# One decode block on one core: smaller K/V tiles, attention finished in two halves, MLP weights in per-partition blocks, a result in four rows

## The chip, the cores and the metric

The kernel runs on 1 core of one Trainium2 chip. The metric is the device time of one execution in microseconds (us). A profile's span is shorter than the time of the same execution (kernel before: 211.4 and 213.17 us). All runs are single-core runs and are called fast here unless a run says otherwise; one execution of one experiment (a_gate_flat) was slow and is left out of its time and its ratio, and a_strides has one execution, whose state is unknown.

## The reference

One token goes through an attention block with a K/V cache and a gated MLP, both behind a layernorm:

```python
# x [1,1,640]; k_cache, v_cache [1,32,4096,128]; wq [640,4096]; wo [4096,640]
# w_gate, w_up [640,1728]; w_down [1728,640]; all bf16
q = layernorm(x) @ wq                          # 32 heads of 128
p = softmax(q . k_cache / sqrt(128))           # per head, 4096 positions
h = x + (p . v_cache) @ wo
h2 = h + (gelu(layernorm(h) @ w_gate) * (layernorm(h) @ w_up)) @ w_down
```

The two caches are 67 MB of the 84 MB that have to come from memory.

## The kernel before

Eight groups of four heads. For each group one 4 MB tile of K and one of V are loaded into three slots in turn. VectorE multiplies K by q, TensorE folds the products (a matmul with the identity adds up slices), VectorE reduces, ScalarE takes the exponentials, TensorE multiplies by V. Below are parts; `...` marks cuts.

```python
for G in range(NG):                      # NG = 8
    for c in range(2):                   # two 64-row pieces of the K tile
        ...                              # VectorE: prod[c] = K piece * q
        for b in range(16): e.matmul(ps_f[c], id_b, prod[:, c, :, 8*b:8*b+8], ...)   # fold
    load_tile(2 * G + 3, consumed[2 * G])
    for c in range(2): ...               # VectorE reduce_sum, then 4 exponentials on ScalarE
    for c in range(2): ...               # TensorE: 64 matmuls with V
    load_tile(2 * G + 4, consumed[2 * G + 1])

d_wo = dma(arena, A_wo "(p i) n -> p (i n)")                 # after all of K and V
d_wg = dma(wg_sb, B_w_gate "(c p) n -> p c n")               # rows of 3456 bytes
d_wu = dma(wu_sb, B_w_up   "(c p) n -> p c n")
d_wd = [..., dma(wd_sb[:, 0:9], ...), dma(wd_sb[:, 9:13], ...)]   # rows of 1280 bytes
...                                                          # normalise; aP = attention, spread
def proj(e):
    for c in range(5):
        for i in range(32):
            e.matmul(ps_p[:, c:c+1], wo_sb[:, i, c*128:(c+1)*128], aP[:, i:i+1], ...)
...                                                          # h = x + projection; layernorm
e.matmul(ps[0:k, m:m+1], w[:, c, m*128:m*128+k], hlnT[:, c:c+1], ...)     # gate, then up
def resid(e): ...                        # 6 matmuls put h into two rows of 320 columns
def down(ms, last):
    for m in ms:
        for b in range(2):
            e.matmul(ps_d[b][0:1, 0:320], hm[0:k, m:m+1], wd_sb[0:k, m, 320*b:320*b+320], ...)
```

The softmax here doesn't subtract the row's maximum and nothing guards it: scores larger than these inputs give would overflow.

Of the kernel before, what the change touches and what calls it, by code (L numbers as in the profile page):

```python
# [5 lines left out]
FP32 = mybir.dt.float32  # L6
BF16 = mybir.dt.bfloat16
ALU = mybir.AluOpType
ACTF = mybir.ActivationFunctionType
AX = mybir.AxisListType  # L10

D = 640
H = 32
DH = 128
SK = 4096
DF = 1728
# [4 lines left out]
NG = 8  # L21
NSLOT = 3
# [69 lines left out]
def bass_sequential_preLN__gqa_block_cached__glu_gated_geglu__decode_kernel(nc, A_x, A_k_cache, A_v_cache, A_wq, A_wo, B_x, B_w_gate, B_w_up, B_w_down, out):  # L92
    sb = lambda name, shape, dt: nc.alloc_sbuf_tensor(name, shape, dt)
    SLOT = 2 * 5 * DF
    slots = [sb("slot%d" % i, [128, SLOT], BF16) for i in range(NSLOT)]
    arena = sb("arena", [128, 5 * 4096], BF16)
    prod = sb("prod", [128, 2, 64, DH], BF16)
    qb = sb("qb", [128, NG, DH], BF16)
    sc = sb("sc", [128, 2, 64], FP32)
    p_bd = sb("p_bd", [128, 2, 128, 4], BF16)  # L100
    RS = sb("RS", [128, 2, H], FP32)
    x_row = sb("x_row", [1, D], BF16)
    out_row = sb("out_row", [1, D], BF16)
    xx = sb("xx", [128, 10], FP32)
# [4 lines left out]
    hT = sb("hT", [128, 5], FP32)  # L109
    hlnT = sb("hlnT", [128, 5], BF16)  # L110
    rz = sb("rz", [128, H], FP32)
    attnN = sb("attnN", [128, H], BF16)
    aT = sb("aT", [32, 128], BF16)
    aP = sb("aP", [128, 32], BF16)
    sel = sb("sel", [32, 4, 128], BF16)
# [8 lines left out]
    ones_b = sb("ones_b", [128, 512], BF16)  # L124
# [7 lines left out]
    ps_o = bank[2]  # L132
    ps_q = [bank[3], bank[4]]
    ps_d = [bank[3], bank[4]]
# [5 lines left out]
    wo_sb = arena[:, :].rearrange("p (i n) -> p i n", i=32)  # L140
    tile = lambda n: slots[n % NSLOT][:, 0:128 * DH].rearrange("p (g d) -> p g d", d=DH)
# [14 lines left out]
    landed = {}  # L156

    def load_tile(n, *deps):
        src = A_k_cache if n % 2 == 0 else A_v_cache
        g = n // 2  # L160
        src = src[0, 4 * g:4 * g + 4, :, :].rearrange("h (p r) d -> (h p) (r d)", p=32)
        landed[n] = P.dma("sync", slots[n % NSLOT][:, 0:128 * DH], src, *deps)

    for n in range(NSLOT):
        load_tile(n)
# [11 lines left out]
    c_sel = GP(lambda e: e.affine_select(sel[:, :, :], ones_b[0:32, :].rearrange("p (a b) -> p a b", a=4),  # L177
                                         pattern=[[-1, 4], [1, 128]], compare_op=ALU.is_equal,
                                         fill=0.0, base=0, channel_multiplier=-4), c_onesb)
# [4 lines left out]
    def x_cols(e):  # L184
        for c in range(5):
            e.matmul(ps_s[:, c:c + 1], x_row[0:1, c::5], one_bf[0:1, 0:1], start=True, stop=True)
        for c in range(5):
            i = e.matmul(ps_s[:, 5 + c:6 + c], x_row[0:1, c * 128:(c + 1) * 128], one_bf[0:1, 0:1],
                         start=True, stop=True)
        return i  # L190
    xt = T(x_cols, d_x, c_one)
    xc = V(lambda e: e.tensor_copy(xx[:, :], ps_s[:, 0:10]), xt)

    def layernorm(src, ev, out_fn, rd_stats=None):
# [11 lines left out]
    xl = layernorm(xx[:, 0:5], xc, lambda e: e.tensor_scalar(  # L206
        xlnB[:, :, :], xx[:, 0:5].unsqueeze(2).to_broadcast([128, 5, 32]), ln[:, 0:1], ln[:, 4:5],
# [18 lines left out]

    folds, reds, exps, pvs = {}, {}, {}, {}
    consumed = {}
    for G in range(NG):
        kt = tile(2 * G)  # L230
        vt = tile(2 * G + 1)
        for c in range(2):
            t = 2 * G + c
            m = V(lambda e, c=c, G=G, kt=kt: e.tensor_tensor(  # L234
                out=prod[:, c, :, :], in0=kt[:, 64 * c:64 * c + 64, :],
                in1=qb[:, G, :].unsqueeze(1).to_broadcast([128, 64, DH]), op=ALU.mult),
                landed[2 * G], qa, qc, folds.get(t - 2))
            consumed[2 * G] = m

            def fold(e, c=c):  # L240
                for b in range(16):
                    i = e.matmul(ps_f[c][:, :], id_b[:, :], prod[:, c, :, 8 * b:8 * b + 8],  # L242
                                 start=(b == 0), stop=(b == 15))
                return i
            folds[t] = T(fold, m, c_idb, reds.get(t - 2))
        if 2 * G + 3 < 16:
            load_tile(2 * G + 3, consumed[2 * G])
        for c in range(2):
            t = 2 * G + c
            reds[t] = V(lambda e, c=c: e.reduce_sum(  # L250
                sc[:, c, :], ps_f[c][:, :].rearrange("p (g d) -> p g d", d=8), axis=AX.X),
                folds[t], exps.get(t - 2))
            for j in range(4):
                x = A(lambda e, c=c, j=j, G=G: e.activation(  # L254
                    p_bd[32 * j:32 * j + 32, G % 2, 64 * c:64 * c + 64, j], sc[32 * j:32 * j + 32, c, :], ACTF.Exp,
                    bias=zero_t[32 * j:32 * j + 32, 0:1], scale=INV_SQRT_DH,
                    accum_out=RS[32 * j:32 * j + 32, c, 4 * G + j:4 * G + j + 1]),
                    reds[t], pvs.get(t - 4), c_pbd, c_rs, c_eps)
            exps[t] = x
        for c in range(2):  # L260
            t = 2 * G + c

            def pv(e, c=c, G=G, vt=vt):
                for g in range(64 * c, 64 * c + 64):
                    i = e.matmul(ps_o[:, 4 * G:4 * G + 4], vt[:, g, :], p_bd[:, G % 2, g, :],  # L265
                                 start=(g == 0), stop=(g == 127))
                return i
            pvs[t] = T(pv, exps[t], landed[2 * G + 1])
        consumed[2 * G + 1] = pvs[2 * G + 1]
        if 2 * G + 4 < 16:  # L270
            load_tile(2 * G + 4, consumed[2 * G + 1])


    d_wo = P.dma("sync", arena[:, :], A_wo[:, :].rearrange("(p i) n -> p (i n)", i=32), qd)
    sl = slots[16 % NSLOT]
    wg_sb = sl[:, 0:5 * DF].rearrange("p (c n) -> p c n", c=5)
    wu_sb = sl[:, 5 * DF:10 * DF].rearrange("p (c n) -> p c n", c=5)
    d_wg = P.dma("sync", wg_sb, B_w_gate[:, :].rearrange("(c p) n -> p c n", p=128), consumed[13])
    d_wu = P.dma("sync", wu_sb, B_w_up[:, :].rearrange("(c p) n -> p c n", p=128))
    sl2 = slots[17 % NSLOT]  # L280
    wd_sb = sl2[:, 0:14 * D].rearrange("p (c n) -> p c n", c=14)
    wd_v = B_w_down[0:1664, :].rearrange("(c p) n -> p c n", p=128)
    d_wd = [P.dma("sync", wd_sb[0:64, 13, :], B_w_down[1664:1728, :], consumed[14]),
# [3 lines left out]

    def zsum(e):
        e.matmul(ps_z[:, 0:H], ones_f[:, :], RS[:, 0, :], start=True, stop=False)
        return e.matmul(ps_z[:, 0:H], ones_f[:, :], RS[:, 1, :], start=False, stop=True)  # L290
    z = T(zsum, exps[15])
    V(lambda e: e.memset(ps_g[64:128, 13:14], 0.0), reds[15])
    V(lambda e: e.memset(ps_u[64:128, 13:14], 0.0), reds[15])
    z1 = V(lambda e: e.reciprocal(rz[:, :], ps_z[:, 0:H]), z)
    z2 = V(lambda e: e.tensor_mul(attnN[:, :], ps_o[:, 0:H], rz[:, :]), z1, pvs[15])
    ps_t = ps_z[0:32, 64:128].bitcast(BF16)
    z3 = T(lambda e: e.transpose(ps_t, attnN[:, :], id_b[:, :]), z2)
    z4 = V(lambda e: e.tensor_copy(aT[:, :], ps_t), z3)

    def spread(e):  # L300
        for q in range(4):
            i = e.matmul(ps_p[:, 8:40], sel[:, q, :], aT[:, 32 * q:32 * q + 32], start=(q == 0), stop=(q == 3))
        return i
    z5 = T(spread, z4, c_sel)
    z6 = V(lambda e: e.tensor_copy(aP[:, :], ps_p[:, 8:40]), z5)

    def proj(e):
        for c in range(5):
            for i in range(32):
                r = e.matmul(ps_p[:, c:c + 1], wo_sb[:, i, c * 128:(c + 1) * 128], aP[:, i:i + 1],  # L310
                             start=(i == 0), stop=(i == 31))
        return r
    pr = T(proj, z6, d_wo)
    h = V(lambda e: e.tensor_add(hT[:, :], xx[:, 5:10], ps_p[:, 0:5]), pr)  # L314
    hl = layernorm(hT[:, :], h, lambda e: e.tensor_scalar(  # L315
        hlnT[:, :], hT[:, :], ln[:, 0:1], ln[:, 4:5], ALU.subtract, ALU.mult))


    def glu(ps, w):
        def fn(e):  # L320
            for m in range(14):
                k = 128 if m < 13 else 64
                for c in range(5):
                    i = e.matmul(ps[0:k, m:m + 1], w[:, c, m * 128:m * 128 + k], hlnT[:, c:c + 1],  # L324
                                 start=(c == 0), stop=(c == 4))
            return i
        return fn
    ga = T(glu(ps_g, wg_sb), hl, d_wg)
    up = T(glu(ps_u, wu_sb), d_wu)

    def resid(e):
        for (c, lo, hi, b) in ((0, 0, 128, 0), (1, 0, 128, 0), (2, 0, 64, 0), (2, 64, 128, 1), (3, 0, 128, 1), (4, 0, 128, 1)):
            o = c * 128 + lo - 320 * b
            i = e.matmul(ps_d[b][0:1, o:o + hi - lo], hT[:, c:c + 1], id_f[:, lo:hi],  # L334
                         start=(o == 0), stop=False, skip_group_check=True)
        return i
    T(resid, c_idf, h)
# [56 lines left out]
```

## Time and profile before

| | before |
|---|---|
| time, median of 4 runs | 212.28 us (211.7 to 212.78) |
| span of the profiled run | 211.4 us |
| DMA queue 1 | 84.23 MB |
| TensorE / VectorE / ScalarE busy | 59% / 41% / 15% |

The page of the kernel before: the span with its instructions, and the shares that the engines and the DMA have in the chain of waits.

```profile
span 211.4 us, 3675 instructions
...
DMA 58%; PE 24%; DVE 10%; issue 4%; ACT 3%; SPq 1%
```

Windows of the same kernel. The columns are: stretch, its length, busy time of TensorE, its weight loads, VectorE, ScalarE and GpSimd with instruction counts, granted TensorE clock, DMA share, GB/s.

```profile
core 0: us, PE busy (x) PEld busy (x) DVE busy (x) ACT busy (x) POOL busy (x), PEclk, DMA share, GB/s
20.00:40.00 20.00, 10.20 (x95) 5.18 (x96) 10.14 (x4) 2.39 (x11) 0.00 (x0) 1.00 0.98 424
...
202.00:204.00 2.00, 2.00 (x12) 0.84 (x10) 0.00 (x0) 0.00 (x0) 0.00 (x0) 0.50 0.04 10
```

From 20 to 40 us, as in all of the loop, the DMA engines have no idle time (share 0.98); after 202 us next to nothing arrives.

TensorE's timeline (start, length, engine, line, operation, out<-in, shape; in brackets the idle time before it and what ended it): output projection (L310), gate and up (L324), residual (L334), down projection (L353).

```profile
186.06 4.30 PE L310 MATMUL bank<-aP,arena 128*128 128x1 bf16 x156 [1.31 <-DMA arena<-in_A_wo_dram]
192.47 0.27 PE L310 MATMUL bank<-aP,arena 128*128 128x1 bf16 x4 [2.12 <-issue]
...
195.53 3.70 PE L324 MATMUL bank<-hlnT,slot 128*128 128x1 bf16 x121 [1.49 <-DVE hlnT L315]
200.27 0.86 PE L324 MATMUL bank<-hlnT,slot 128*128 128x1 bf16 x19 [1.04 <-issue]
201.06 2.29 PE L334 MATMUL bank<-id_f,hT 128*1 128x128 f32 x12
203.28 5.99 PE L353 MATMUL bank<-slot,hm 64*1 64x320 bf16 x28
```

The down projection is 28 matmuls of one output row in 6.0 us, and it starts when the weights are already there. That is the tail without DMA that the change goes for. The two gaps marked `issue` (2.12 and 1.04 us) are ones in which TensorE waited for nothing that the profile's page shows.

### The profile page before, as it was taken

What the parts mean: (1) busy time and instruction counts of PE and PEld (TensorE: products, weight loads), DVE (VectorE), ACT (ScalarE), POOL (GpSimd) and SP (SyncE); (2) the same over time, 40 slices, a digit from 0 to 9 for tenths busy, and PEclk for the clock granted to TensorE, in tenths of its full rate; (3) what the DMA queues carried; (4) which work ended last, traced back from release to release, by engine and by line L of the source; (5) the groups of instructions that cost most, each with busy time, mean ns of one, the idle gap of its engine ahead of it and who ended that gap; (6) DMA issues with size and microseconds to landing.
All of it is one profiled execution on the core that took longest, in us unless ns stands there. A gap on an engine that the chain in (4) does not pass through costs nothing.

```text
span 211.4 us, 3675 instructions
## 1 busy us (share of the span) xinstructions
PE 125.3 (59%) x1683; PEld 72.8 (34%) x1683; DVE 87.6 (41%) x66; ACT 31.7 (15%) x136; POOL 2.8 (1%) x10
## 2 busy tenths in 40 slices
PE   2304039815970796099449807960994199671896
PEld 1101014611460245035314602450353035571752
DVE  2001295139416911972295159218720962102110
ACT  3001002400330033004202300330042005101000
POOL 5000000000000000000000000000000000000000
PEclk9999999965995599559659955995595569555558
DMA  6999999999999999999999999999999999899800
GB/s 242 443 443 446 409 453 434 403 474 415 394 478 412 409 465 415 414 453 422 425 440 422 431 437 415 446 434 406 447 434 419 440 402 490 348 418 380 301 23 0
DMA packets 5843, 84.46 MB, mean 400 GB/s; under 512 B 386, under 2 KB 2116, under 8 KB 3396
## 3 DMA queue, kind: packets, MB, share of 16 engines
q1 hardware_dynamic: 5826, 84.23, 94.0%
q8 instruction: 13, 0.21, 0.4%
q14 instruction: 2, 0.02, 0.0%
q10 hardware_dynamic: 2, 0.00, 0.0%
HBM read 84.23 MB, written 0.00 MB: 399 GB/s over the span
## 4 chain that ended last, share of the span: by engine, by line
DMA 58%; PE 24%; DVE 10%; issue 4%; ACT 3%; SPq 1%
DMA slot<-in_A_k_cache_dram 42%; DMA arena<-in_A_wo_dram 16%; PE bank L242 13%; DVE prod L234 8%; PE bank L353 3%; PE bank L265 3%; ACT p_bd L254 2%; PE bank L310 2%; PE bank L324 2%; PE bank L334 1%; DVE sc L250 1%; SPq L50 1%; PE bank L198 0%; DVE out_row L359 0%; ACT ln L202 0%
## 5 line engine op out<-in xcount | busy, mean ns | idle before, releaser
L242 PE MATMUL bank<-prod,id_b 128*128 128x512 bf16 x256 | 73.0, 456 | 55.6 <-DVE prod L234 55.6
L234 DVE TENSOR_TENSOR prod<-slot,qb 128x8192 bf16<-128x8192 bf16 x16 | 70.1, 4422 | 44.7 <-DMA slot<-in_A_k_cache_dram 44.7
L242 PEld LDWEIGHTS bank<-prod,id_b 128*128 128x128 bf16 x256 | 28.3, 114 | 97.8 <-DVE prod L234 57.1
L254 ACT ACTIVATE p_bd<-sc,zero_t 32x64 bf16<-32x64 f32 x64 | 27.7, 433 | 133.4 <-DVE sc L250 132.7
L265 PE MATMUL bank<-p_bd,slot 128*128 128x4 bf16 x1024 | 28.5, 165 | 8.1 <-ACT p_bd L254 8.1
L265 PEld LDWEIGHTS bank<-p_bd,slot 128*128 128x128 bf16 x1024 | 27.8, 97 | 10.7 <-ACT p_bd L254 8.8
L250 DVE TENSOR_REDUCE sc<-bank 128x64 f32<-128x512 f32 x16 | 11.1, 692 | 33.6 <-PE bank L242 33.6
L254 ACT ACTIVATION_READ_ACCUMULATOR p_bd<-sc,zero_t 32x1 f32 x64 | 11.8, 184 | 0.0
L218 PE MATMUL bank<-arena,xlnB 128*32 128x512 bf16 x40 | 4.7, 628 | 9.8 <-DMA arena<-in_A_wq_dram 9.8
L310 PE MATMUL bank<-aP,arena 128*128 128x1 bf16 x160 | 4.6, 165 | 3.4 <-issue 2.1
L324 PE MATMUL bank<-hlnT,slot 128*128 128x1 bf16 (+1 forms) x140 | 4.6, 168 | 2.5 <-DVE hlnT L315 1.5
L224 DVE CAST qb<-bank 128x512 bf16<-128x512 f32 x1 | 0.7, 691 | 13.0 <-PE bank L218 13.0
L353 PE MATMUL bank<-slot,hm 128*1 128x320 bf16 (+1 forms) x28 | 6.0, 388 | 0.0
L310 PEld LDWEIGHTS bank<-aP,arena 128*128 128x128 bf16 x160 | 4.4, 104 | 3.6 <-issue 3.6
L218 PEld LDWEIGHTS bank<-arena,xlnB 128*32 128x32 bf16 x40 | 1.3, 133 | 12.4 <-DMA arena<-in_A_wq_dram 6.2
L324 PEld LDWEIGHTS bank<-hlnT,slot 128*128 128x128 bf16 (+1 forms) x140 | 4.4, 107 | 2.7 <-DVE hlnT L315 1.6
L353 PEld LDWEIGHTS bank<-slot,hm 128*1 128x1 bf16 (+1 forms) x28 | 2.7, 102 | 3.4 <-issue 1.0
L359 DVE CAST out_row<-bank 1x320 bf16<-1x320 f32 x1 | 0.5, 479 | 7.4 <-PE bank L353 7.4
L314 DVE TENSOR_TENSOR hT<-xx,bank 128x5 f32<-128x5 f32 x1 | 0.2, 162 | 7.8 <-PE bank L310 7.8
L202 ACT ACTIVATE ln<-ln,eps_t 128x1 f32<-128x1 f32 x2 | 0.6, 294 | 15.9 <-DVE ln L200 15.9
L225 ACT CAST qb<-bank 128x512 bf16<-128x512 f32 x1 | 0.6, 586 | 13.4 <-PE bank L218 13.4
L334 PE MATMUL bank<-id_f,hT 128*1 128x128 f32 (+1 forms) x12 | 2.3, 378 | 0.0
(57 smaller groups left out, 19.0 us busy)
## 6 DMA issues: line engine op xcount, KB each, us to landing
slot<-in_A_k_cache_dram SPq DMA_DIRECT2D x8, 4096.0 KB, 21.8
slot<-in_A_v_cache_dram SPq DMA_DIRECT2D x8, 4096.0 KB, 20.6
arena<-in_A_wo_dram SPq DMA_DIRECT2D x1, 5120.0 KB, 33.4
arena<-in_A_wq_dram SPq DMA_DIRECT2D x1, 3072.0 KB, 14.3
slot<-in_B_w_gate_dram SPq DMA_DIRECT2D x1, 2160.0 KB, 29.4
slot<-in_B_w_up_dram SPq DMA_DIRECT2D x1, 2160.0 KB, 34.8
arena<-in_A_wq_dram SPq DMA_DIRECT2D x1, 2048.0 KB, 7.5
slot<-in_B_w_down_dram SPq DMA_DIRECT2D x1, 1440.0 KB, 16.6
```

Source lines behind the costliest of these rows:

```text
L50: ev = self.op(eng, lambda e: e.dma_start(out, in_), *deps, dma=True)
L218: i = e.matmul(ps_q[hf][32 * j:32 * j + 32, :], xlnB[:, c, :], wq_j[:, c, j, 4 * hf:4 * hf + 4, :], start=(c == 0), stop=(c == 4))
L224: qa = V(lambda e: e.tensor_copy(qb[:, 0:4, :].rearrange("p g d -> p (g d)"), ps_q[0][:, :]), qd)
L234: m = V(lambda e, c=c, G=G, kt=kt: e.tensor_tensor(out=prod[:, c, :, :], in0=kt[:, 64 * c:64 * c + 64, :], in1=qb[:, G, :].unsqueeze(1).to ...
L242: i = e.matmul(ps_f[c][:, :], id_b[:, :], prod[:, c, :, 8 * b:8 * b + 8], start=(b == 0), stop=(b == 15))
L250: reds[t] = V(lambda e, c=c: e.reduce_sum(sc[:, c, :], ps_f[c][:, :].rearrange("p (g d) -> p g d", d=8), axis=AX.X), folds[t], exps.get(t ...
L254: x = A(lambda e, c=c, j=j, G=G: e.activation(p_bd[32 * j:32 * j + 32, G % 2, 64 * c:64 * c + 64, j], sc[32 * j:32 * j + 32, c, :], ACTF.E ...
L265: i = e.matmul(ps_o[:, 4 * G:4 * G + 4], vt[:, g, :], p_bd[:, G % 2, g, :], start=(g == 0), stop=(g == 127))
L310: r = e.matmul(ps_p[:, c:c + 1], wo_sb[:, i, c * 128:(c + 1) * 128], aP[:, i:i + 1], start=(i == 0), stop=(i == 31))
L324: i = e.matmul(ps[0:k, m:m + 1], w[:, c, m * 128:m * 128 + k], hlnT[:, c:c + 1], start=(c == 0), stop=(c == 4))
L334: i = e.matmul(ps_d[b][0:1, o:o + hi - lo], hT[:, c:c + 1], id_f[:, lo:hi], start=(o == 0), stop=False, skip_group_check=True)
L353: i = e.matmul(ps_d[b][0:1, 0:320], hm[0:k, m:m + 1], wd_sb[0:k, m, 320 * b:320 * b + 320], start=False, stop=(last and m == ms[-1]), skip ...
```

## The change

It intends to (1) load K/V in 2 MB tiles into 6 slots and score in 32-row pieces, so that slots come free sooner; (2) finish heads 0 to 15 while heads 16 to 31 are still running, and project them before the end, for which half of wo is loaded before the last group; (3) load the MLP weights as one long run per partition, which changes which rows lie on which partition, and so which columns a weight load must take; (4) compute the result in four strips of 160 columns on four partitions. The diff, cut to its core:

```diff
-NSLOT = 3
+NSLOT = 6
+            if n == NT - 4:                      # before the last group's four tiles
+                d_wo[0] = P.dma("sync", arena[:, 0:16 * D], A_wo[0:2048, :]..., qd)
 ... score_tile: two 32-row pieces; VectorE's order is mul, mul, reduce, reduce per tile
+        if G == NG - 1:
+            pr0 = proj_half(0, a0)               # TensorE: after the folds, before the V matmuls
+        if G == 3:
+            a0 = finish_half(0)
-                r = e.matmul(ps_p[:, c:c + 1], wo_sb[:, i, c * 128:(c + 1) * 128], aP[:, i:i + 1],
+                    r = e.matmul(ps_p[:, c:c + 1], wo_sb[:, t, i, c::5], aP[:, t, i:i + 1],
-    d_wg = P.dma("sync", wg_sb, B_w_gate[:, :].rearrange("(c p) n -> p c n", p=128), consumed[13])
+    d_wg = P.dma("sync", wg_sb, B_w_gate[:, :].rearrange("(p c) n -> p c n", c=5), consumed[NT - NSLOT])
 ... w_up and w_down alike
-                    i = e.matmul(ps[0:k, m:m + 1], w[:, c, m * 128:m * 128 + k], hlnT[:, c:c + 1], ...)
+                    ws = w[:, c, m:1664:13] if m < 13 else w[:, c, 1664:1728]
+                    i = e.matmul(ps[0:k, m:m + 1], ws, hlnT[:, c:c + 1], ...)
-                for b in range(2):
-                    i = e.matmul(ps_d[b][0:1, 0:320], hm[0:k, m:m + 1], wd_sb[0:k, m, 320 * b:320 * b + 320], ...)
+                for q in range(4):
+                    i = e.matmul(ps_d[32 * q:32 * q + 1, 0:160], hm[0:k, m:m + 1],
+                                 wd_sb[0:k, m, 160 * q:160 * q + 160], ...)
 ... residual through hX in the same strips; one multiply instead of four small operations after up
```

## The prediction

> **What bounds it now.** The DMA stream. The page's header shows 84.46 MB at a mean of 400 GB/s; windows from 20 to 160 us a DMA share of 0.98 to 1.02 at 422 to 439 GB/s; the chain of waits is 58% DMA. Three 4 MB slots already keep the queue full, so PE (59%) and DVE (41%) have slack in the loop. The last weight packets land near 203 us (windows: 111 GB/s at 200 to 202, 10 at 202 to 204). From there to 211.4 us is a tail without DMA: the down projection, 28 matmuls of 1x320 in series, 5.94 us at a granted clock of 0.5; a copy, 0.48; the result's store, about 1.6.
>
> **The stream after.** Bytes and order stay nearly the same. From the packets' own durations (16 KB 611 ns, 32 KB 1214, so about 8.5 ns fixed each; 3456 B 136; 1280 B 56 to 61):
> - K/V packets of 16 KB instead of 32: 128 more per DMA engine, about +1.2 us.
> - MLP weights in per-partition blocks (17, 11.5 and 5 KB instead of 3456 and 1280 B): about -1.9 us.
> The stream ends some 0.7 us earlier, estimated at 202.5 us. Six 2 MB slots hold the same 12 MB; smaller pieces shorten latency off the critical path, so I give the loop nothing.
>
> **The tail after.** Half the output projection moves before the last V pieces; after the second half of wo lands (about 187 us) come 80 matmuls (27.6 ns each in the trace, 2.2 us), layernorm 2.8, gate 2.0, all before w_up lands near 197.5; up 2.0, one multiply. So PE should wait for weights, no longer the weights for PE. The down projection has the same columns, as four strips of 160 in four column groups. [...] the q projection's 40 matmuls of 512 columns, over four groups, take about 117 ns each against 427 ns for unpacked ones of that width at the slow clock. I estimate 2 us for the first 40, 0.8 us for the last 16, which alone follow the last landing; then one copy, about 0.3, and the store, 1.6. Span about 205.3, measured about 1 us more: 206.2 us, 3% less.
>
> **Costs.** Twice as many exponentials (0.44 us each, 7 us per group of 19.5 us), half-size multiplies, twice the reduces (0.69 us each): all fit. Weights are loaded with a column stride of 5 or 13 elements. [...] the trace has the stride-5 loads of x at about 45 ns a pair[...].
>
> **Signs.** Right: DMA share near 1.0 up to about 202 us; 16 KB packets of 611 ns; chain ending in the last w_down landing, then down, copy, store in about 3 us; down near 50 ns a matmul; weight-load pairs of wo and gate/up near 28 ns. Wrong: pairs of 50 ns or more; down still serial (over 4 us); DMA share under 0.95 in the loop.
>
> **What would make it wrong.** Strided weight loads at 100 ns a pair would add some 10 us and lose everything. Instruction-fetch stalls, if that is what the gaps of 2.1 and 1.0 us in the tail are (PE waited for nothing visible), could fall into the end: +1 to 2 us. A smaller spread between DMA engines at the end would give 2 us more.

Three passages are cut from it, where marked: two general statements, on matmuls in column groups and on weight loads with a column step, for which no trace of this case is the source, and a comparison that the trace does not bear out (point 3 under "Why the prediction was wrong"). The 117 ns were taken at a granted clock of 1.00 and the 427 ns at 0.50; at 1.00 the unpacked matmuls of that width start every 216 ns in the same trace. The 2 us in the last sentence fit the DMA share of 0.81 from 198 to 200 us and 0.30 from 200 to 202 us: the idle shares of 0.19 and 0.70, times 2 us each, make 1.8.

## More of the kernel before

VectorE's timeline at the last group (start, length, engine, line, operation, out<-in, shape; in brackets the idle time before it and what ended it): the last K tile lands at 163.85 us, and the attention result is ready for the output projection at 185.0.

```profile
163.85 8.76 DVE L234 TENSOR_TENSOR prod<-slot,qb 128x8192 bf16<-128x8192 bf16 x2 [5.80 <-DMA slot<-in_A_k_cache_dram]
...
184.79 0.19 DVE L305 CAST aP<-bank 128x32 bf16<-128x32 f32 x1 [0.38 <-PE bank L302]
```

## The result

The changed kernel takes 214.73 us (median of 4 runs, 214.39 to 215.44), against 212.28 for the kernel before. The ratio is 1.012 (95% interval 1.008 to 1.016): slower, though by less than 2%. Ratios in this document are the mean time of one kernel's fast runs over that of the other's of the same rounds, so they are not quite the ratios of the medians quoted.

The page of the changed kernel, the same lines:

```profile
span 213.2 us, 3941 instructions
...
DMA 50%; PE 34%; DVE 11%; issue 2%; SPq 1%; ACT 0%
```

Its windows, with the same columns:

```profile
20.00:40.00 20.00, 13.21 (x122) 6.34 (x123) 11.66 (x8) 6.56 (x32) 0.00 (x0) 0.91 1.01 431
...
202.00:204.00 2.00, 2.00 (x35) 1.97 (x33) 0.25 (x2) 0.00 (x0) 0.00 (x0) 0.50 0.05 20
```

The loop is as busy with DMA as before (1.01), TensorE's part of the chain has grown from 24% to 34%, and the stream ends about as before. The last piece of w_down landed 17.2 us after its issue in the kernel before and 31.1 us after it in the changed one (the table of DMA issues), which is 202.7 and 203.2 us on the two spans. VectorE's timeline at the last group:

```profile
166.29 4.49 DVE L246 TENSOR_TENSOR prod<-slot,qb 128x4096 bf16<-128x4096 bf16 x2 [9.42 <-DMA slot<-in_A_k_cache_dram]
...
175.20 0.69 DVE L259 TENSOR_REDUCE sc<-bank 128x32 f32<-128x512 f32 x1 [2.24 <-PE bank L254]
175.81 4.48 DVE L246 TENSOR_TENSOR prod<-slot,qb 128x4096 bf16<-128x4096 bf16 x2
...
192.90 0.17 DVE L300 CAST aP<-bank 128x16 bf16<-128x16 f32 x1 [0.47 <-PE bank L297]
```

TensorE's timeline from there: folds of the last group (L254), output projection (L306), V (L279), gate and up (L355), down (L383).

```profile
168.64 6.53 PE L254 MATMUL bank<-prod,id_b 128*128 128x512 bf16 x16 [8.24 <-DVE prod L246]
178.15 5.20 PE L254 MATMUL bank<-prod,id_b 128*128 128x512 bf16 x16 [2.98 <-DVE prod L246]
183.19 3.32 PE L306 MATMUL bank<-aP,arena 128*128 128x1 bf16 x80
186.37 2.04 PE L279 MATMUL bank<-p_bd,slot 128*128 128x4 bf16 x75
189.35 1.55 PE L279 MATMUL bank<-p_bd,slot 128*128 128x4 bf16 x53 [0.93 <-issue]
...
193.13 3.36 PE L306 MATMUL bank<-aP,arena 128*128 128x1 bf16 x80 [0.27 <-DVE aP L300]
...
199.28 8.78 PE L355 MATMUL bank<-hlnT,slot 128*128 128x1 bf16 x140 [1.49 <-DVE hlnT L343]
...
208.63 2.13 PE L383 MATMUL bank<-slot,hm 64*1 64x160 bf16 x56
```

The two kernels can be laid side by side, stage by stage, from these lines and their neighbours (us):

| stage | before | after | difference |
|---|---|---|---|
| attention ready (end of aP) | 185.0 | 193.1 | +8.1 |
| wait for wo | 1.1 | 0.1 | -1.0 |
| output projection still to do, with its gaps | 6.7 | 3.4 | -3.3 |
| layernorm | 2.8 | 2.8 | 0 |
| gate and up, with gaps | 5.6 | 8.8 | +3.2 |
| residual, last multiplies | 2.2 | 0.6 | -1.6 |
| down | 6.0 | 2.2 | -3.8 |
| copy, store, end | 2.1 | 2.4 | +0.3 |

The differences add up to +1.9, and the spans differ by 1.8. So the tail gained nearly 10 us where the change meant it to, and lost 11.3 in two places: attention ends later, and gate and up take longer. In the changed kernel the last landing in the chain is that of the last group's first K piece (166.3 us); from there it runs through TensorE, with short pieces of VectorE and ScalarE, to the end. At the last landing (203.2 us) it had not yet finished gate and up.

### The profile page after: what moved, and what is told of

The parts are those of the page before. It is cut to its first block, busy times and chain, and to the rows that moved or that the text cites. A ratio compares the mean times of both kernels' runs of the same rounds, so it can differ in the third digit from the quotient of the medians.

```text
span 213.2 us, 3941 instructions
## 1 busy us (share of the span) xinstructions
PE 141.3 (66%) x1715; PEld 79.6 (37%) x1715; DVE 101.8 (48%) x106; ACT 55.8 (26%) x263; POOL 3.8 (2%) x10
## 4 chain that ended last, share of the span: by engine, by line
DMA 50%; PE 34%; DVE 11%; issue 2%; SPq 1%; ACT 0%
DMA slot<-in_A_k_cache_dram 50%; PE bank L254 21%; DVE prod L246 10%; PE bank L355 4%; PE bank L279 4%; PE bank L306 3%; SPq L50 1%; PE bank L383 1%; PE bank L364 0%; PE bank L209 0%; PE bank L288 0%; PE bank L297 0%; DVE out_sb L390 0%; ACT ln L214 0%; ACT ln L213 0%
## 5 line engine op out<-in xcount | busy, mean ns | idle before, releaser
L254 PE MATMUL bank<-prod,id_b 128*128 128x512 bf16 x256 | 88.2, 520 | 45.1 <-DVE prod L246 45.1
L246 DVE TENSOR_TENSOR prod<-slot,qb 128x4096 bf16<-128x4096 bf16 x32 | 71.8, 2285 | 21.9 <-DMA slot<-in_A_k_cache_dram 21.9
L263 ACT ACTIVATE p_bd<-sc,zero_t 32x32 bf16<-32x32 f32 x128 | 46.3, 362 | 114.3 <-DVE sc L259 112.8
L254 PEld LDWEIGHTS bank<-prod,id_b 128*128 128x128 bf16 x256 | 31.0, 127 | 99.7 <-DVE prod L246 51.3
L259 DVE TENSOR_REDUCE sc<-bank 128x32 f32<-128x512 f32 x32 | 22.1, 691 | 44.5 <-PE bank L254 44.5
L279 PE MATMUL bank<-p_bd,slot 128*128 128x4 bf16 x1024 | 28.5, 165 | 7.3 <-ACT p_bd L263 6.3
L279 PEld LDWEIGHTS bank<-p_bd,slot 128*128 128x128 bf16 x1024 | 27.8, 97 | 9.7 <-ACT p_bd L263 6.9
L263 ACT ACTIVATION_READ_ACCUMULATOR p_bd<-sc,zero_t 32x1 f32 x128 | 23.5, 184 | 0.0
L355 PE MATMUL bank<-hlnT,slot 128*128 128x1 bf16 (+1 forms) x140 | 8.8, 199 | 1.5 <-DVE hlnT L343 1.5
L355 PEld LDWEIGHTS bank<-hlnT,slot 128*128 128x128 bf16 (+1 forms) x140 | 8.7, 161 | 1.6 <-DVE hlnT L343 1.6
L306 PE MATMUL bank<-aP,arena 128*128 128x1 bf16 x160 | 6.7, 179 | 0.3 <-DVE aP L300 0.3
L306 PEld LDWEIGHTS bank<-aP,arena 128*128 128x128 bf16 x160 | 6.6, 131 | 0.6 <-DVE aP L300 0.4
L383 PE MATMUL bank<-slot,hm 128*1 128x160 bf16 (+1 forms) x56 | 2.1, 331 | 0.0
```

Source lines behind the costliest of these rows:

```text
L246: m = V(lambda e, s=s, u=u: e.tensor_tensor(out=prod[:, s % 4, :, :], in0=kt[:, 32 * u:32 * u + 32, :], in1=qb[:, G, :].unsqueeze(1).to_br ...
L254: i = e.matmul(ps_f[s % 2][:, :], id_b[:, :], prod[:, s % 4, :, 16 * b:16 * b + 16], start=(b == 0), stop=(b == 7))
L259: reds[s] = V(lambda e, s=s: e.reduce_sum(sc[:, s % 4, :], ps_f[s % 2][:, :].rearrange("p (g d) -> p g d", d=16), axis=AX.X), folds[s], ex ...
L263: x = A(lambda e, s=s, j=j: e.activation(p_bd[32 * j:32 * j + 32, G % 2, 32 * (s % 4):32 * (s % 4) + 32, j], sc[32 * j:32 * j + 32, s % 4, ...
L279: i = e.matmul(po[:, o:o + 4], vt[:, g, :], p_bd[:, G % 2, 64 * k + g, :], start=(k == 0 and g == 0), stop=(k == 1 and g == 63))
L306: r = e.matmul(ps_p[:, c:c + 1], wo_sb[:, t, i, c::5], aP[:, t, i:i + 1], start=(t == 0 and c == 0 and i == 0), stop=(t == 1 and i == 15), ...
```

## The experiments

My theory had two parts. First, weight loads with a column step are slow. Second, attention ends late because of what the change put in front of its last steps: half of wo in the DMA order, half of the projection in TensorE's order, and VectorE's order of multiplies and reduces. The rivals: the weight loads are slow for another reason (the clock of 0.5, the transfers arriving beside them); the small pieces' own work is what delays attention; and the blocks are worth more than the strides cost.

| run | against the kernel before | time (us) | ratio, 95% interval |
|---|---|---|---|
| changed kernel | | 214.73 | 1.012 (1.008 to 1.016) |
| a_gate_flat | after, no step in gate/up | 211.58 (three fast runs) | 0.997 (0.992 to 1.002) |
| a_all_flat | after, no step at all | 210.34 | 0.989 (0.983 to 0.995) |
| a_strides | after, six steps | 216.61 | one run, state unknown |
| a_half_early | after, half projection earlier | 210.25 | 0.992 (0.985 to 0.999) |
| a_wo_late | after, wo behind K/V | 209.50 | 0.987 (0.983 to 0.991) |
| a_dve_order | after, VectorE order | 210.44 | 0.992 (0.989 to 0.995) |
| a_no_blocks | after, blocks undone | 209.38 | 0.987 (0.984 to 0.991) |
| a_three | three repairs together | 208.91 | 0.984 (0.981 to 0.987) |
| b_strips | before, strips alone | 207.85 | 0.980 (0.976 to 0.984) |
| b_strips_wo2 | b_strips, wo in two pieces | 207.63 | 0.978 (0.976 to 0.981) |
| b_strips_wo2_blocks | that, gate/up in blocks | 207.50 | 0.977 (0.975 to 0.980) |

The kernel before had medians of 212.2 to 212.6 us in these rounds.

### Weight loads with a step: a_gate_flat, a_all_flat, a_strides

```diff
-                    ws = w[:, c, m:1664:13] if m < 13 else w[:, c, 1664:1728]
+                    ws = w[:, c, 128 * m:128 * m + k]          # a_gate_flat and a_all_flat
-                    r = e.matmul(ps_p[:, c:c + 1], wo_sb[:, t, i, c::5], ...)
+                    r = e.matmul(ps_p[:, c:c + 1], wo_sb[:, t, i, 128 * c:128 * c + 128], ...)   # a_all_flat
```

These two and the next one compute a wrong result. The comparison with the reference passed them all the same, so its pass proves nothing about such columns.

> The changed kernel, but gate and up load their weights with neighbouring columns instead of every 13th (the result is wrong on purpose; transfers and their order are the same). If the stride makes the weight loads slow: the 140 pairs take about 3.9 us instead of 8.8, the measured time falls by about 4.9 us to 210. If the slow clock or the transfers that arrive beside them make them slow: still near 63 ns a pair, 214.7 us.

> As the run before, and the output projection too loads neighbouring columns instead of every 5th (wrong result on purpose). Stride theory: its 80 pairs per half take 2.2 us instead of 3.36, both halves lie on the path, so another 2.3 us: about 207.5 us, unless the last weights (landed 203.2 us after the start) now end the wait. Rival: 214.7 us.

Measured: 211.58 us (the median of the three fast runs; the first run, which holds the profile, was slow at 229.96 us and isn't used) and 210.34 us. TensorE's timeline of a_all_flat, in part: the second piece of the last V matmuls, then gate and up.

```profile
189.17 1.56 PE L279 MATMUL bank<-p_bd,slot 128*128 128x4 bf16 x53 [2.43 <-issue]
...
198.85 3.38 PE L355 MATMUL bank<-hlnT,slot 128*128 128x1 bf16 x109 [1.49 <-DVE hlnT L343]
202.98 1.19 PE L355 MATMUL bank<-hlnT,slot 128*128 128x1 bf16 x31 [0.75 <-issue]
```

In a_all_flat gate and up take 4.6 us plus a gap of 0.75, instead of 8.8, and the second half of the projection 2.5 us plus a gap of 0.65, instead of 3.4. So it is the step: the edit leaves the transfers and the order as they were, and the granted clock at gate and up is 0.50 in the traces of the changed kernel and of a_all_flat. The changed kernel's own trace speaks against both rivals too. The first half of its projection ran at a clock of 1.00 and took 3.32 us, the second at 0.50 and took 3.36. And at gate and up each 2 us from 200 to 208 us hold 35 to 37 matmuls, while the DMA share falls from 0.40 to 0.00. The time fell by 3.2 and 4.4 us rather than the expected 4.9 and 7.2. Part of that was my sizing. Even flat, the 140 loads of gate and up cost 33 ns each, because the ten with 64 columns are slower (149 against 104 ns a load in the groups). The other part is the `issue` gaps: two are new, and the one inside the last V matmuls grew from 0.93 to 2.43 us. It swallowed the first half's saving of 1.2 us before the end of attention (192.9 us in this trace, 193.1 in the changed kernel).

> The disputed cost by itself: the changed kernel with six column steps in its weight loads (wrong result on purpose): 2 in the first half of the output projection, 3 in the second, 8 and 16 in the halves of gate, 32 and 64 in the halves of up. Known: 27.6 ns a pair at step 1, 42 at 5, 63 at 13. If the cost grows with the bytes spanned, 64 is far over 63 ns; if it is one of access per element, it levels off near the value at 13 to 16; if the step itself does not matter, all are alike.

```diff
+    def cols(flat, s, o):
+        return flat[:, o:o + 127 * s + 1:s]
 ... proj half 0: s = 2, half 1: s = 3; gate: s = 8, then 16; up: s = 32, then 64
```

The chain of waits of a_strides in order of time (start, length, what, how many), cut to the projection's and the MLP's groups:

```profile
183.12 1.98 PE bank L311 x80
...
193.73 1.87 PE bank L318 x64
...
199.90 2.28 PE bank L366 x35
202.17 2.18 PE bank L372 x35
204.36 2.24 PE bank L378 x35
206.59 3.14 PE bank L384 x35
```

Divided by the counts: step 2 costs 25 ns a pair of weight load and matmul, step 3 29, step 8 65, step 16 62, step 32 64 and step 64 90 ns. With step 1 at 27 to 29, step 5 at 42 and step 13 at 63 from the other traces, the curve is flat up to 3 elements, climbs between 3 and 8, is level from 8 to 32, and climbs once more at 64. (The granted clock was 1.00 at step 2 and 0.50 at the others. At 1.00 the 80 pairs with step 1 in a_all_flat's first half take 1.98 us, 25 ns each too, so step 2 costs nothing.) Neither of my two pictures had all of this. What makes a step cost this is not shown: this is one execution, and no run varied the element size. The rise at 64 is left unexplained too.

### What delays the end of attention: a_half_early, a_wo_late, a_dve_order

```diff
     for G in range(NG):
+        if G == NG - 1:
+            pr0 = proj_half(0, a0)          # a_half_early: ahead of the last group's folds
         for k in range(2):
             score_tile(G, k)
             ...
-        if G == NG - 1:
-            pr0 = proj_half(0, a0)
```

> The changed kernel, with the first half of the output projection put before the last group's score work on TensorE, where it idles, instead of before the last attention-times-V matmuls. If those 3.3 us in TensorE's order delay the end of attention: the last attention matmul ends near 187.7 instead of 190.9 us, time 211.5. If attention waits only for the exponentials (done at 185.8): no more than 0.5 us less, 214.3.

TensorE's timeline of a_half_early:

```profile
160.36 2.54 PE L306 MATMUL bank<-aP,arena 128*128 128x1 bf16 x60
...
168.40 5.05 PE L254 MATMUL bank<-prod,id_b 128*128 128x512 bf16 x16 [4.01 <-DVE prod L246]
176.43 1.90 PE L254 MATMUL bank<-prod,id_b 128*128 128x512 bf16 x8 [2.98 <-DVE prod L246]
178.63 1.90 PE L254 MATMUL bank<-prod,id_b 128*128 128x512 bf16 x8 [0.30 <-DVE prod L246]
...
183.03 1.77 PE L279 MATMUL bank<-p_bd,slot 128*128 128x4 bf16 x64 [0.90 <-ACT p_bd L263]
```

Measured 210.25 us, 4.5 us less, where 3.2 was expected. The four runs are far apart (209.22, 209.27, 211.23 and 212.32 us), and the trace is of the 209.27 one, so it shows the effect at its larger end. The projection now fills a stretch in which TensorE waited for K. The last V matmuls end at 184.8 instead of 190.9, and attention is ready at 186.8 instead of 193.1. The extra comes from the folds: those of the first K piece take 5.05 us instead of 6.53, and those of the second 1.90 + 1.90 us instead of 5.20 in all. The idle time before the last group's folds is 4.0 us instead of 8.2 and the granted clock is 1.00 from 172 to 180 us, where the changed kernel has 0.68 (to 176) and 0.74. In this pair of traces the shorter idle time goes with the higher clock. The other traces do not sort that way: the first 16 folds take 5.74 us after 2.93 us of idle time in a_wo_late, and 5.99 us after 9.13 us in a_all_flat. So what raised the clock is not shown. From 198 us on, the chain of this run follows the landing of w_up.

```diff
-            if n == NT - 4:
-                d_wo[0] = P.dma(...)        # a_wo_late: issued after the last K/V tile instead,
+    d_wo[0] = P.dma(...)                    # and projected after attention
```

> The changed kernel, with the first half of wo loaded after the last K/V pieces instead of before them, and its projection put behind the end of attention. If the 2.6 MB in front of the last group delay the end of attention: the last group's K pieces land 6 us earlier (160.2 and 165.1 us), attention is done near 184 instead of 193, the projection near 190.8 instead of 196.5: about 209 us. If attention's end is set by the small pieces' own work and not by the landing: 213 us or more.

The timeline of a_wo_late, in part: first multiply of the last group, end of attention, the two halves of the projection.

```profile
158.90 4.50 DVE L244 TENSOR_TENSOR prod<-slot,qb 128x4096 bf16<-128x4096 bf16 x2 [4.12 <-DMA slot<-in_A_k_cache_dram]
...
180.08 0.17 DVE L298 CAST aP<-bank 128x16 bf16<-128x16 f32 x1 [0.47 <-PE bank L295]
...
181.11 3.36 PE L304 MATMUL bank<-aP,arena 128*128 128x1 bf16 x80 [1.06 <-DMA arena<-in_A_wo_dram]
...
187.52 3.33 PE L304 MATMUL bank<-aP,arena 128*128 128x1 bf16 x80 [3.05 <-DMA arena<-in_A_wo_dram]
```

Measured 209.50 us, expected 209. The last group starts at 158.90 instead of 166.29, and attention is ready at 180.3 instead of 193.1. TensorE then waits 1.06 and 3.05 us for the two halves of wo. This run also takes the half projection out of the way of the V matmuls, which by a_half_early is worth up to 6.3 of the 12.8 us. The other 6.5 fit the 2.6 MB of wo at 426 GB/s (6.1 us), the changed kernel's rate from 160 to 168 us. The small pieces' own work is not the cause: with this order attention is ready earlier than in the kernel before (185.0).

The order per tile and per group, in words rather than code:

```diff
-    mul 0, mul 1, reduce 0, reduce 1, mul 2, mul 3, reduce 2, reduce 3
+    mul 0, mul 1, mul 2, reduce 0, mul 3, reduce 1, reduce 2, reduce 3     # a_dve_order, last group only
```

> The changed kernel, with VectorE's order in the last group alone altered: the multiplies of the second K piece go ahead of the first piece's reduces. In the changed kernel that piece lands at 171.2 us and its multiply starts at 175.8, behind a reduce that waits for TensorE's folds. If that order costs on the path: the folds end near 180.3 instead of 183.4, time 211.8. If not: 214.7.

The timeline of a_dve_order, in part: the folds, the first multiply of the second K piece, the half projection.

```profile
168.46 10.19 PE L258 MATMUL bank<-prod,id_b 128*128 128x512 bf16 x32 [8.30 <-DVE prod L247]
...
170.99 2.29 DVE L247 TENSOR_TENSOR prod<-slot,qb 128x4096 bf16<-128x4096 bf16 x1 [0.39 <-DMA slot<-in_A_k_cache_dram]
...
178.48 3.33 PE L324 MATMUL bank<-aP,arena 128*128 128x1 bf16 x80
```

Measured 210.44 us, expected 211.8. The second K piece is multiplied when it lands, at 170.99, instead of at 175.81. The folds run in one go of 10.2 us and end at 178.7 instead of 183.4, more than the 3 us that I had expected.

### The blocks: a_no_blocks

> The changed kernel with the per-partition blocks undone: the MLP weights with the rows of before (1280 and 3456 B runs), so that every weight load takes neighbouring columns; the result is right. If the blocks cost more in strided loads than they give in transfers: about 210.3 us, as with the loads flattened and the blocks kept (210.34), since the stream's end moves by only some 0.65 us. If the blocks' transfers are worth more than that: 212 us or more.

```diff
-    wd_v = B_w_down[0:1664, :].rearrange("(p c) n -> p c n", c=13)
+    wd_v = B_w_down[0:1664, :].rearrange("(c p) n -> p c n", c=13)
 ... w_gate and w_up alike; every weight load takes neighbouring columns again
```

Measured 209.38 us, 5.3 us less than the changed kernel, and the result is right. Weight loads are back near 29 to 33 ns. The last piece of w_down lands at 204.1 us instead of 203.2; over all traces with 2 MB tiles that is 203.9 and 204.1 without the blocks (this run and a_three) and 203.2 to 203.6 with them (six traces). So the blocks gave about 0.7 us of transfer, behind which the kernel was not waiting, and took over 5 us on the chain.

### Do the repairs add up: a_three

> Three repairs of the changed kernel together: blocks undone (alone it gave -5.3 us), first half of the output projection early on TensorE (-4.5), VectorE's order in the last group (-4.3). If all three shorten one chain that is floored by the landing of the last weights (near 204 us in the kernel without blocks): about 208.7 us, hardly below the best of the three alone (209.4). If they added up: near 200.6 us.

Measured 208.91 us, as the floor theory has it. TensorE's timeline of a_three: projection, gate, up, down.

```profile
187.38 2.27 PE L327 MATMUL bank<-aP,arena 128*128 128x1 bf16 x80 [1.38 <-DMA arena<-in_A_wo_dram]
...
192.66 2.23 PE L378 MATMUL bank<-hlnT,slot 128*128 128x1 bf16 x70 [1.71 <-DMA slot<-in_B_w_gate_dram]
198.19 2.24 PE L378 MATMUL bank<-hlnT,slot 128*128 128x1 bf16 x70 [3.30 <-DMA slot<-in_B_w_up_dram]
...
202.46 2.23 PE L406 MATMUL bank<-slot,hm 64*1 64x160 bf16 x56 [1.38 <-DMA slot<-in_B_w_down_dram]
```

Every one of these stages now waits for a landing, with 1.38 to 3.30 us of idle time before it. The last 16 weight loads of down wait for the last piece of w_down:

```profile
203.99 0.36 PEld L406 LDWEIGHTS bank<-slot,hm 128*1 128x1 bf16 x16 [0.27 <-DMA slot<-in_B_w_down_dram]
```

### The strips alone: b_strips, b_strips_wo2, b_strips_wo2_blocks

> The kernel before with one part of the change: the down projection and the residual as four strips of 160 columns on four partitions, the result stored as 4 rows. If the serial down projection was the tail of the kernel before and strips run side by side: down 2.1 us instead of 5.9 and the residual 0.7 instead of 2.2, the time falls by about 5 us to 207. If the last landing (202.7 us) or a fetch stall comes in between: 208 to 210.

The edit is the strip part of the change's diff put into the kernel before, with hX laid out for that kernel's order of columns. Down in the timeline of b_strips:

```profile
201.58 2.13 PE L357 MATMUL bank<-slot,hm 64*1 64x160 bf16 x56 [0.18 <-DVE hm L350]
```

Measured 207.85 us, 2.0% faster than the kernel before (0.976 to 0.984; whether it is more or less than 2% this interval leaves open). This is 4.7 us less, and the same down projection that cost 6.0 us takes 2.1.

> The kernel before with the strips (207.85 us), wo loaded and projected in two pieces after the last V (neighbouring columns), and only one multiply left after up. If the strips' kernel still waits for TensorE by about 1 us at the end (its last multiply ends at 201.5 us, w_down's last piece lands at 202.3): the last multiply ends near 199.5, the end follows the landing, about 207.0 us. If the landing already ends it: 207.8.

```diff
+    d_wo = [P.dma("sync", arena[:, 16*D*t:16*D*t + 16*D], wo_v[:, 16*D*t:16*D*t + 16*D], qd) for t in range(2)]
+    T(proj(0), z6, d_wo[0]);  pr = T(proj(1), d_wo[1])
 ... hm = (g_t * t1) * ps_u, so that one multiply is left after up
```

Measured 207.63 us: 0.2 less, in another set of rounds and within the intervals, so nearer to the case in which the landing already ends it. The same weight loads as in the last line of a_three wait for the same transfer here, 1.3 us earlier:

```profile
202.65 0.36 PEld L362 LDWEIGHTS bank<-slot,hm 128*1 128x1 bf16 x16 [0.29 <-DMA slot<-in_B_w_down_dram]
```

Both kernels load the MLP weights in the same rows and differ in the K/V tiles (2 and 4 MB) and the place of wo. The difference is near what I had put on the 16 KB packets (+1.2 us), though no run changes the packets alone.

> As the run before, and gate and up alone loaded in per-partition blocks, which needs the column step of 5 in the output projection (42 instead of 28 ns a pair, 2.3 us) but not the step of 13. If there is slack before w_up lands, the strided projection costs nothing and the stream ends some 0.6 us earlier: about 206.4 us. If there is none: 208 us or more.

```diff
-    rearrange("(c p) n -> p c n", p=128)     # w_gate, w_up
+    rearrange("(p c) n -> p c n", p=128)     # and the projection takes columns c::5
```

Measured 207.50 us, against 207.63 within intervals that overlap: no gain that can be told apart. The strided projection costs nothing here: it takes 6.56 us without a gap, where the flat one of b_strips_wo2 takes 4.59 us and a gap of 1.88. But the stream does not end earlier either, and the last weight loads wait for it just as long:

```profile
202.71 0.36 PEld L362 LDWEIGHTS bank<-slot,hm 128*1 128x1 bf16 x16 [0.29 <-DMA slot<-in_B_w_down_dram]
```

So 207.5 us is the fastest that was run; it beats both kernels, and the strips do nearly all of it.

## Why the prediction was wrong

Predicted were 206.2 us, measured 214.73. Point by point:

1. **Bound by the DMA stream, with a full queue in the loop: right.** The share is 1.01 in the loop of the changed kernel.
2. **"The stream ends some 0.7 us earlier": wrong by about 1.2 us.** It ended 0.5 us later. The +1.2 us for 16 KB packets was about right (1.3 between a_three and b_strips_wo2, which differ in the place of wo as well). The -1.9 us for the blocks was too much: about 0.7 us for all three weights, and none that could be seen for gate and up alone.
3. **"Weight-load pairs of wo and gate/up near 28 ns": this step failed.** They took 42 (step 5) and 63 ns (step 13), 4.2 us more for gate and up than flat ones and 0.9 to 1.2 for each half of the projection. The 28 ns were those of loads of neighbouring columns; that a step would leave them alone was my assumption. My control in the trace was misread: I had put the stride-5 loads of x and the contiguous ones after them at 45 ns a pair alike. By their starts in the trace of the kernel before, the matmuls of the five strided pairs follow each other every 40 ns after the first, and those of the five contiguous ones every 26 to 27 ns (L186 and L188, 2.1 to 2.4 us, granted clock 1.00). So the control had shown that a step costs something.
4. **"After the second half of wo lands (about 187 us) come 80 matmuls": this step failed too.** wo did land near 187, but attention was not ready until 193.1. I had costed the projection and never the end of attention itself. Three things the change moved stood before it: 2.6 MB of wo ahead of the last K/V (about 6 us at the loop's rate), half of the projection in TensorE's order ahead of the V matmuls (3.3 us), and reduces that wait for TensorE ahead of multiplies whose data are there (4.8 us). Put right one at a time they gave 5.2, 4.5 and 4.3 us, where the 5.2 of a_wo_late holds the first two together.
5. **"PE should wait for weights, no longer the weights for PE": wrong,** as a consequence of 3 and 4. It comes true in a_three.
6. **Down projection near 50 ns a matmul, 2.8 us: right that the strips run side by side.** In the changed kernel four matmuls start within 6 to 10 ns, and from the third such group on the next four come 133 to 134 ns later (granted clock 0.50). It took 38 ns a matmul, 2.1 us for 56 of them, where 28 of 320 columns had taken 6.0; with the residual it gained 5.4 us.
7. **What I had named as a risk, strided loads,** was the right one. I put it at 100 ns and 10 us "and lose everything"; 42 and 63 ns together with the later end of attention were enough.

The repairs do not add up (5.3 + 4.5 + 4.3 would be 14.1, a_three gives 5.8), because they shorten one chain above one floor: the last landing plus about 3 us. The `issue` gaps, the last open point, are not explained on the profile's page, but the list of DMA packets in the traces tells more. From 155 us on, the twelve traces used here (all but that of a_gate_flat) hold 17 such gaps, of 0.38 to 2.96 us. All fall at the same four places in TensorE's stream, after 2497, 2753, 3010 and 3265 recorded instructions, 255 to 257 apart. Each ends 2.35 to 2.64 us after a 16 KB packet has started on DMA queue 8, whose packets the profile marks `instruction` (13 in each of the two kernels' traces). Where the packet starts early enough there is no gap: the kernel before passes the second place at 186.8 us, 4.4 us after its packet. From these times the gaps may be instruction fetches that come too late, the risk that the prediction named; that is an inference, and no run changed the length of the program to test it. Faster weight loads run into them: the changed kernel's strided loads pass the third and fourth place without a gap, the flat ones of a_all_flat wait 0.65 and 0.75 us there.

## What to carry to other kernels

In this DMA-bound kernel a new order of transfers gained nothing in the loop (DMA share 0.98 and 1.01), so what decided was the chain from the last landing that attention needs to the end; write down when each link of that chain is ready, not only when its weights land. Whatever is moved "early" takes a place in some engine's or queue's order, and it should be put where that engine idles, not in front of the last critical step. A layout that lengthens the runs of a transfer may hand a stride to the weight loads (here 42 ns a pair at step 5 and 63 at step 13, against 27 to 29 at step 1): check the time of such pairs in a trace, from start to start.
